# Gate and up operands of ten blocks made by GpSimd during attention and kept in DRAM, in a transformer block of attention and a gated MLP

## The chip, the cores and the metric

The kernel runs on one core of a Trainium2 chip. The metric is the device time of one execution in microseconds (us). The kernel before takes 2934.76 us, the median of three runs (2932.86 to 2934.86). The engines are called PE (matmul; PEld is its weight load), DVE (vector), ACT (scalar), POOL (GpSimd) and SP (which issues most DMAs here).

## The reference, cut to what matters

One sequence of 2048 rows with 576 features goes through a transformer block whose two normalizations are modulated by a condition `c`.

```python
mod = (silu(c) @ w_mod).reshape(1, 6, 1, -1)           # sa, ca, ga, sb, cb, gb
h = layernorm(x) * (1 + ca) + sa
x = x + ga * attention(h, wqkv, wo)                    # 32 heads of 18 features, softmax
h = layernorm(x) * (1 + cb) + sb
x = x + gb * ((sigmoid(h @ w_gate) * (h @ w_up)) @ w_down)   # 4608 hidden features
return x
```

All is float32. The kernel gets near that precision on PE's float32r format by splitting operands into a high part and a low part (the rest after rounding) and adding three products.

## The kernel before, in words

**Projections** (up to about 235 us of the span). Rows are normalized and modulated, and q, k and v are projected. q and k are kept in DRAM as high and low parts.

**Attention** is written as 32 units of 16 steps. A unit is a pair of heads and one half of the query rows; a step `kt` is one tile of 128 keys. Each step has four score products (L877), four exps on ACT (L881), the value products of earlier steps (L501) and four score products for the maxima (L411) of a later unit, each reduced by DVE (L415). PE's order is written out by hand here (`STEPS`), while the other engines' queues are filled by a scheduler from the program's order and its dependences. At the end of a unit ACT copies the accumulated values into `oT` (L515), PE transposes them, ACT copies them back into `oT` (L540) and POOL multiplies them by the reciprocals into `Oa`, or `big` in the second half (L544). `oT` has a single buffer. So L515 of a unit waits for L544 of the unit before.

Beside this, side work is handed out in turns: generators (`first_rows`, `down_parts`, `last_rows_project`) that are advanced at certain steps. `down_parts` runs from step 64 to step 240: for each of the 18 blocks of 256 hidden features POOL loads a piece of `w_down`, multiplies it by the gate `gb`, splits it and stores it in DRAM (`wds`), L779 to L801. Its loads are `paced`: they wait for the exp of the step in which they are issued. From step 240 on, the first half's rows are projected, normalized and made into operands of the MLP, with much work for POOL; the units from there on also hold the matmuls of the output projection.

**Modulation.** In units 1 and 3 the second and third part of `w_mod` are loaded, into the tiles `big` and `w0`, by `load_mod`, and used eight steps later by `modulate`.

**The MLP** runs over two halves of 1024 rows, 18 blocks of 256 hidden features each and seven products per block in the order 1, 6, 2, 7, 5, 4, 3 (`ORDER`): a Strassen-like scheme in which seven products of quarter blocks take the place of eight. Each product multiplies a weight operand (gate and up together) with a prepared row operand `X`. A weight operand is made in `weights_operand`, three products ahead (`LOOK`). In the first half `load_block` loads the raw weights; POOL makes the sums S1 to S3 (L959), ACT rounds (L970), DVE subtracts (L971, and L972 for the last 64 rows), and the result is stored in DRAM (`ws`, L973). In the second half it is loaded from `ws`. For block 0 the raw weights are loaded late in attention, and the first three operands are made behind attention's end. After two of the seven products of a block the down products of the block before are run (L1015) and added to the rows in `Oa` by DVE (L1019).

Also in the first half, `last_rows` works on the second half's rows in turns, at every odd n of the 126 products from n = 5 on: output projection, normalization, and the operands of the second half. It uses all engines, and loads pieces back from DRAM (`hs`) that it has stored.

Of the kernel before, what the change touches and what calls it, by code (L numbers as in the profile page):

```python
# [43 lines left out]
NB = F // 256  # L44
LAG = 2
# [6 lines left out]
def tile_block(ctx, tc, x_in, wqkv, wo, w_gate, w_up, w_down, c_in, w_mod, out):  # L52
# [33 lines left out]
    def load_mod(a, b, i):  # L86

        cols = slice(2 * D * i, 2 * D * (i + 1))
        for t in range(0, 4, 2):
            rows = slice(t * P, (t + 2) * P)  # L90
            nc.sync.dma_start(a[:, t : t + 2, :], w_mod[rows, cols].rearrange("(t p) c -> p t c", p=P))
        nc.sync.dma_start(b[0:64, :], w_mod[DM:D, cols])
        return [a[:, t, :] for t in range(4)] + [b]
# [218 lines left out]
    with tc.tile_pool(name="ln", bufs=2) as ln:  # L312
# [23 lines left out]
        with tc.tile_pool(name="wmp", bufs=1) as wmp:  # L336
            zs = normalized(0)
            wm = wmp.tile([P, 5, 2 * D], F32, name="wm")
            wm = load_mod(wm[:, 0:4, :], wm[:, 4, :], 0)
# [468 lines left out]
    def load_block(pool, b, k, tied=None):  # L808
# [4 lines left out]
        raw = pool.tile([P, 2, 3, 256], F32, name=f"raw{k}", bufs=1 + k)  # L813
        queue = nc.gpsimd if tied else nc.sync
# [10 lines left out]
        return raw  # L825
# [18 lines left out]
    downs = down_parts()  # L844
    for u in range(UNITS):
# [6 lines left out]
        for kt in range(NT):  # L852
# [31 lines left out]
            if u in (1, 3):  # L884
                if kt == 2:
                    a = big.tile([P, 8, 640], F32, name="big")
                    a = a.rearrange("p a b -> p (a b)")[:, 0 : 8 * D].rearrange("p (t c) -> p t c", t=4)
                    b = slots.tile([P, 2560], F32, name="w0")[:, 0 : 2 * D]
                    mods = load_mod(a, b, 1 + u // 2)
                    row = slots.tile([P, 2560], F32, name="w1")[:, 0:384]  # L890
# [4 lines left out]
            if 4 * NT <= step < FROM0 and step % 2 == 0:  # L895
                next(downs, None)
            if step == FROM0:
                for _ in downs:
                    pass
# [5 lines left out]
            if u == 30 and kt == 7:  # L905
                first = [load_block(raws, 0, k, paced) for k in range(2)]
# [4 lines left out]
            if u == UNITS - 1 and kt == 9:  # L911
# [5 lines left out]
                for i in range(2):  # L917
                    X[5 + i] = both[:, i]
                    load_x(5 + i)
    while pending:  # L920
        values()
# [20 lines left out]
    def weights_operand(st, k):  # L942
# [3 lines left out]
        kept = ws[st["b"], ORDER.index(k)]  # L946
        flat = w.rearrange("p v a c -> p (v a c)").bitcast(F32)
        if st["half"] == 1:
            nc.sync.dma_start(flat, kept.bitcast(F32))
# [11 lines left out]
        if k == 6:  # L961
            put("S1", A21, A22, ALU.add)
            put("S2", st["S1"], A11, ALU.subtract)
            put("S3", A11, A21, ALU.subtract)
# [7 lines left out]
        nc.vector.tensor_sub(w[64:P, :, 2, :], src[64:P, :, 2, :], w[64:P, :, 2, :].bitcast(F32))  # L972
# [258 lines left out]
```

## Time and profile before

| what | value |
|---|---|
| median of three runs | 2934.76 us |
| the profiled execution | 2936.12 us |
| its span, first to last instruction | 2934.3 us |
| busy: PE, DVE, ACT, POOL | 98%, 79%, 51%, 21% of the span |
| mean granted TensorE clock | 0.994 |
| first copies `oT` (L515) at steps 17, 65, 241 | 278.00, 408.05, 857.88 us |
| last copy `oT` | 1599.21 us |
| first product of the MLP | 1602.88 us |
| copy of the second half's first product | 2287.20 us |

In the rows of the profile a line names the place in the kernel, then engine, operation, `out<-in` with the tiles' names, shapes and the count; behind the bar stand the total busy time in us and the mean of one in ns, then the idle time ahead of these instructions and what ended it. In an answer by time the first column is the start in us and the second the duration; square brackets hold idle time ahead and its releaser. In an answer by stretches the columns are the stretch, its length, then the busy time and number of instructions of PE, PEld, DVE, ACT and POOL, the granted clock, the DMA engines' share and GB/s. A row on waits gives us in total, times and the longest. A row on DMA issues ends with the median us from issue to landing.

### The profile page before, as it was taken

Reading aid. Unit: us, or ns where it says so; the run is one execution under the profiler, and the core shown is the slowest. Engines: PE = TensorE matmul, PEld = TensorE weight load, DVE = VectorE, ACT = ScalarE, POOL = GpSimd, SP = SyncE. Lnnn points to the kernel's source line nnn. Section 1 sums busy time; section 2 is a strip of 40 time slices with the busy share of each in tenths; the row PEclk is TensorE's granted clock in tenths of the full one; section 3 lists DMA queues with packets and bytes.
Section 4 is the critical chain, followed back from the end, with each engine's and each line's share of the span. In section 5 each row is a group of like instructions: output and inputs, shape, how many; then the busy total and the mean of one; then the engine's idle time right before and its main releaser. Section 6 shows DMA issues by size and latency. Waiting matters only on the chain.

```text
span 2934.3 us, 46129 instructions
## 1 busy us (share of the span) xinstructions
PE 2867.2 (98%) x17141; PEld 1884.6 (64%) x17141; DVE 2305.1 (79%) x4021; ACT 1497.6 (51%) x2779; POOL 614.7 (21%) x793
## 2 busy tenths in 40 slices
PE   7999999999999999999999999998999999999999
PEld 6974333333334443443443788887888888888888
DVE  7278999999999999999992778888777555555555
ACT  3217778888887678878778333333332111111111
POOL 2001024444213110661102222233221100000000
PEclk9999999999999999999999999999999999999999
DMA  5333113333212110221125866686556854444443
GB/s 170 119 138 115 63 58 134 126 116 112 83 50 70 31 50 19 95 92 60 48 78 185 280 217 231 232 278 242 204 201 225 303 177 168 166 168 169 158 158 137
DMA packets 136089, 420.25 MB, mean 143 GB/s; under 512 B 18805, under 2 KB 56441, under 8 KB 123577
## 3 DMA queue, kind: packets, MB, share of 16 engines
q1 hardware_dynamic: 120472, 338.35, 33.7%
q0 software_dynamic: 15392, 78.95, 7.6%
q8 instruction: 135, 2.21, 0.3%
q14 instruction: 90, 0.73, 0.1%
HBM read 261.13 MB, written 155.59 MB: 142 GB/s over the span
## 4 chain that ended last, share of the span: by engine, by line
PE 85%; DVE 5%; ACT 4%; issue 3%; DMA 2%; SPq 1%; POOL 0%; ACTq 0%; DVEq 0%; POOLq 0%
PE o L501 17%; PE d L1015 14%; PE s L877 13%; PE x L979 13%; PE s L411 9%; PE bg L979 4%; PE bu L979 4%; PE s L267 4%; ACT p L881 3%; PE s L301 2%; PE s L638 2%; DVE w L971 1%; PE s L525 1%; DMA B<-hs 1%; DVE u L1163 0%
## 5 line engine op out<-in xcount | busy, mean ns | idle before, releaser
L415 DVE TENSOR_REDUCE mx<-s 128x1 f32<-128x512 f32 x2048 | 1266.9, 681 | 43.9 <-PE s L411 35.3
L881 ACT ACTIVATE p<-s 128x512 f32<-128x512 f32 x2048 | 1066.9, 607 | 268.7 <-PE s L411 145.4
L411 PE MATMUL s<-k,q 54*128 54x512 f32 x1920 | 658.0, 441 | 2.6 <-ACT p L881 1.0
L877 PE MATMUL s<-q,k 56*128 56x512 f32 x1920 | 581.5, 433 | 6.3 <-ACT p L881 0.4
L877 PEld LDWEIGHTS s<-q,k 56*128 56x128 f32 x1920 | 277.6, 185 | 469.5 <-DVE mx L415 292.6
L501 PE MATMUL o<-p,vaug 128*32 128x512 f32 x4096 | 554.4, 606 | 0.0
L1015 PE MATMUL d<-wd,hh 128*128 128x288 f32 x2304 | 470.9, 298 | 20.9 <-DVE Oa L1019 20.3
L1015 PEld LDWEIGHTS d<-wd,hh 128*128 128x128 f32 x2304 | 375.7, 189 | 35.8 <-DVE Oa L1019 27.2
L411 PEld LDWEIGHTS s<-k,q 54*128 54x128 f32 x1920 | 312.1, 185 | 80.5 <-ACT p L881 37.4
L1019 DVE TENSOR_TENSOR Oa<-Oa,d 128x288 f32<-128x288 f32 x576 | 255.9, 452 | 128.2 <-PE d L1015 123.1
L1015 PE MATMUL d<-wd,hl 128*128 128x288 f32 x1152 | 342.0, 297 | 0.0
L979 PE MATMUL x<-k,w 128*128 128x512 f32 x1008 | 245.5, 394 | 4.7 <-ACT w L970 2.4
L1015 PEld LDWEIGHTS d<-wd,hl 128*128 128x128 f32 x1152 | 218.1, 189 | 0.0
L979 PEld LDWEIGHTS x<-k,w 128*128 128x128 f32 x1008 | 188.8, 190 | 43.2 <-DVE u L1190 3.5
L991 ACT ACTIVATE u<-u 128x512 f32<-128x512 f32 x72 | 45.5, 631 | 318.7 <-DVE u L1179 312.7
L501 PEld LDWEIGHTS o<-p,vaug 128*32 128x32 f32 x4096 | 83.6, 108 | 163.7 <-issue 147.7
L988 ACT ACTIVATE sg<-x 128x512 f32<-128x512 f32 x36 | 21.5, 598 | 309.4 <-PE x L979 309.4
L1021 POOL DMA_DIRECT2D out_dram<-Oa x16 | 8.7, 542 | 606.5 <-DVE Oa L1019 606.5
L979 PE MATMUL x<-big,w 128*128 128x512 f32 x504 | 120.6, 390 | 1.0 <-issue 1.0
L979 PE MATMUL x<-w,w 128*128 128x512 f32 x504 | 121.0, 390 | 0.0
L267 PE MATMUL s<-hT,wq_h 128*128 128x512 f32 x324 | 106.1, 399 | 1.9 <-DVE hT L204 1.2
L979 PEld LDWEIGHTS x<-big,w 128*128 128x128 f32 x504 | 94.3, 188 | 21.0 <-issue 1.4
(221 smaller groups left out, 3345.2 us busy)
## 6 DMA issues: line engine op xcount, KB each, us to landing
ws<-w SPq DMA_DIRECT2D x126, 640.0 KB
w<-ws SPq DMA_DIRECT2D x126, 640.0 KB
wd<-wds SPq DMA_DIRECT2D x36, 1152.0 KB
wds<-w POOLq DMA_DIRECT2D x18, 1152.0 KB, 4.5
k<-qk SPq DMA_DIRECT2D x60, 288.0 KB
qk<-pl SPq DMA_DIRECT2D x32, 512.0 KB
w<-in_B_w_down_dram POOLq DMA_DIRECT2D x18, 576.0 KB, 4.9
q<-qk SPq DMA_DIRECT2D x64, 144.0 KB
```

The lines of the kernel that those rows point to most:

```text
L267: nc.tensor.matmul(acc, w, hT[:, t, cols], start=n == 0, stop=n == len(ts_) - 1)
L301: nc.tensor.matmul(acc[:, 0:HALF], hT[:, k, rows], w, start=n == 0, stop=n == len(ts_) - 1,)
L411: nc.tensor.matmul(sp, qs[rows, qt * P : (qt + 1) * P], ks[rows, kc * 512 : (kc + 1) * 512], start=True, stop=True,)
L415: nc.vector.tensor_reduce(mx[:, h * n + qt, kc : kc + 1], sp, axis=AX.X, op=ALU.max)
L501: nc.tensor.matmul(acc[32 * j : 32 * j + 32, :], vaug[:, kt, (2 * p + h) * VW : (2 * p + h) * VW + 32], probs[2 * c + h], start=kt == 0, s ...
L638: nc.tensor.matmul(acc[:, :HALF], a, w, start=i == 0, stop=i == len(ts_) - 1)
L877: nc.tensor.matmul(sT, ks[rows, kcols], qs[rows, c * 512 : (c + 1) * 512], start=True, stop=True)
L881: state["exp"] = nc.scalar.activation(pr, sT, AF.Exp, scale=SCALE)
L979: nc.tensor.matmul(acc[v], w[:, v, a, :], X[s][:, b, :], start=first and n == 0, stop=n == 6, skip_group_check=not first,)
L991: nc.scalar.activation(t[:, 0:512], t[:, 0:512], AF.Sigmoid)
L1015: nc.tensor.matmul(acc[:, :HALF], a[:, f, rows], w[:, f, cols], start=n == 0, stop=n == 5)
L1019: nc.vector.tensor_add(Oa[:, t, cols], Oa[:, t, cols], acc[:, :HALF])
```

## The change

1. A new generator `operands` makes the seven gate and up operands of blocks 0 to 9 (`AHEAD = 10`) on POOL alone, during attention. Per block it issues eight raw loads from POOL's queue (paced), then in seven turns the sums, the rounding, the two subtractions, and a store to `ws`. All of it lives in one tile `big` with one buffer: raw weights, sum, and one operand `w` that the next turn overwrites. Turns are given at every third step up to step 63 and at three steps of eight from step 64 to 239, 88 turns in all for 80 that hold work.
2. In the MLP's first half, blocks 0 to 9 load their operands from `ws` (`load_operand`), as the second half does. The first three operands of block 0 are loaded in the last unit of attention into the space of the raw weights.
3. Blocks 10 to 17 are made as before, but for the 64-row subtraction, which goes from DVE to POOL, and S3, which is made one operand later.
4. Since `big` is taken, modulation's weights go to the tiles `w0` and `w1` and a temporary tile.
5. `last_rows` gets a turn at two n of three, and two turns without work behind the loads from `hs`.
6. Block 0's down weights are loaded ahead of the MLP's loop.

The core of the diff:

```diff
+AHEAD = 10
...
+    def operands():
+        for b in range(AHEAD):
+            room = big.tile([P, 8, 640], F32, name="big").rearrange("p a b -> p (a b)")
+            raw = [room[:, i * 1536 : (i + 1) * 1536].rearrange("p (v t c) -> p v t c", v=2, t=3) for i in range(2)]
+            S_ = room[:, 3072:3840].rearrange("p (v t c) -> p v t c", v=2, t=3)
+            flat = room[:, 3840:5120]
+            w = flat.rearrange("p (v a c) -> p v a c", v=2, a=5)
+            for k in range(2):
+                fill_block(raw[k], b, k, nc.gpsimd, paced)
+            yield
+            A11, A12 = raw[0][:, :, :, 0:P], raw[1][:, :, :, 0:P]
+            A21, A22 = raw[0][:, :, :, P:256], raw[1][:, :, :, P:256]
+            for k, src, op, a, c in (
+                (5, S_, ALU.add, A21, A22), (6, S_, ALU.subtract, S_, A11),
+                (3, S_, ALU.subtract, A12, S_), (7, S_, ALU.subtract, A11, A21),
+                (1, A11, None, None, None), (2, A12, None, None, None), (4, A22, None, None, None),
+            ):
+                if op is not None:
+                    for v in range(2):
+                        nc.gpsimd.tensor_tensor(S_[:, v], a[:, v], c[:, v], op=op)
+                for v in range(2):
+                    nc.gpsimd.tensor_copy(w[:, v, 0:3, :].bitcast(F32R), src[:, v])
+                nc.gpsimd.tensor_sub(w[:, :, 3:5, :].bitcast(F32R), src[:, :, 0:2, :], w[:, :, 0:2, :])
+                nc.gpsimd.tensor_sub(
+                    w[64:P, :, 2, :].bitcast(F32R), src[64:P, :, 2, :], w[64:P, :, 2, :]
+                )
+                nc.gpsimd.dma_start(ws[b, ORDER.index(k)].bitcast(F32), flat)
+                yield
...
+            if step < 4 * NT and step % 3 == 0 or 4 * NT <= step < FROM0 and (step % 4 == 1 or step % 8 == 3):
+                next(ops, None)
...
-            if u == 30 and kt == 7:
-                first = [load_block(raws, 0, k, paced) for k in range(2)]
...
+                begun = {"b": 0, "half": 0}
+                for i, k in enumerate(ORDER[:LOOK]):
+                    w = raws.tile([P, 1536], F32R, name=f"raw{min(i, 1)}", bufs=1 + min(i, 1))[:, 0:1280]
+                    begun["w", k] = w.rearrange("p (v a c) -> p v a c", v=2, a=5)
+                    load_operand(begun["w", k], 0, k)
...
-        if st["half"] == 1:
-            nc.sync.dma_start(flat, kept.bitcast(F32))
+        if st["half"] == 1 or st["b"] < AHEAD:
+            load_operand(w, st["b"], k)
             return
...
-        nc.vector.tensor_sub(w[64:P, :, 2, :], src[64:P, :, 2, :], w[64:P, :, 2, :].bitcast(F32))
+        nc.gpsimd.tensor_sub(w[64:P, :, 2, :], src[64:P, :, 2, :], w[64:P, :, 2, :].bitcast(F32))
...
+                yield
+                yield
                 yield from operand_parts(1, i, blocks, parts, nc.scalar.copy, nc.vector, nc.sync)
...
-        if n >= 5 and n % 2:
+        if n >= 5 and n % 3:
             next(rows2, None)
```

What the order of the instructions shows, at three places. First POOL in attention before, between the multiplications of one unit (L544) and the next; `w_5235` is the tile in which a block of down weights is worked on:

```order
L544 TENSOR_TENSOR Oa<-oT,rec 128x8x18 x2
L779 DMA w_5235<-in_B_w_down_dram 128x2x576
L794 TENSOR_TENSOR w_5235<-w_5235,gb_b 128x288 x2
L795 CAST w_5235<-w_5235 128x288 x2
L796 TENSOR_TENSOR w_5235<-w_5235 128x288 x2
```

The same engine now, at a later unit; `big` holds the operand's parts, and lines have moved by one:

```order
L848 TENSOR_TENSOR big<-big 128x2x256
L849 TENSOR_TENSOR big<-big 64x2x128
L797 TENSOR_TENSOR w_7284<-w_7284 128x288
L852 DMA ws<-big 128x1280
L845 TENSOR_TENSOR big<-big 128x384 x2
L795 TENSOR_TENSOR w_7284<-w_7284,gb_b 128x288
L796 CAST w_7284<-w_7284 128x288
L797 TENSOR_TENSOR w_7284<-w_7284 128x288
L802 DMA wds<-w_7284 128x2304
L847 CAST big<-big 128x384 x2
```

The operands' instructions stand in one queue with those of the down weights, and a unit's multiplications behind both.

Second, ACT at the beginning of a unit now, with the semaphores that each instruction waits for (L915 is the exp, L881 before):

```order
L915 ACTIVATE p_7031<-s_7029 128x512 [waits PE_49]
L516 COPY oT<-o 128x512 [waits PE_49,Pool_49]
L915 ACTIVATE p_7042<-s_7040 128x512 [waits PE_49,Activation_49]
L915 ACTIVATE p_7052<-s_7050 128x512 [waits PE_49,Activation_49]
L915 ACTIVATE p_7059<-s_7057 128x512 [waits PE_49]
```

Before, the same copy stands at the same place with the same waits; the exps behind it stand in its queue.

Third, SP at the beginning of the MLP before, where it issues the stores of fresh operands and the loads of the next raw weights:

```order
L973 DMA ws<-w 128x1280 [waits DVE_49,DMAHW4_49,PE_49,Activation_49]
L973 DMA ws<-w 128x1280 [waits DVE_49,Activation_49]
L816 DMA raw_20722<-in_B_w_gate_dram 128x2x256 [waits DMASW6_49,DMASW1_49,DMASW7_49,DMASW0_49,Pool_49]
L818 DMA raw_20722<-in_B_w_gate_dram 128x1x256
L816 DMA raw_20722<-in_B_w_up_dram 128x2x256
```

And now:

```order
L969 DMA oend<-last 1024x1x36 [waits DMAHW3_49,DVE_49]
L856 DMA w<-ws 128x1280 x3
L1115 DMA od<-oend 128x4x192 [waits DMAHW0_49,DMAHW3_49,PE_49,Activation_49]
L1116 DMA od<-oend 128x4x64
L1137 DMA xt<-x1p 128x576 [waits DMAHW1_49]
L1137 DMA xt<-x1p 128x576 [waits DMAHW2_49]
```

The stores are gone, and the operands come as loads that wait for no DVE and no ACT.

65 lines of the change are left out of this document (37 added, 28 removed).

## The prediction

> **What bounds the kernel now.** I read the page first, then stages of equal length, then the waits of the matmul engine.
>
> ```profile
> span 2934.3 us, 46129 instructions
> PE 2867.2 (98%) x17141; PEld 1884.6 (64%) x17141; DVE 2305.1 (79%) x4021; ACT 1497.6 (51%) x2779; POOL 614.7 (21%) x793
> ```
>
> ```profile
> 450.00:492.00 42.00, 41.54 (x268) 16.80 (x272) 41.23 (x71) 35.19 (x71) 19.37 (x31) 1.00 0.35 124
> 786.00:828.00 42.00, 41.62 (x271) 16.90 (x268) 41.22 (x70) 34.84 (x70) 0.82 (x2) 1.00 0.11 33
> ```
>
> ```profile
> 1900.00:2000.00 100.00, 91.10 (x484) 79.28 (x483) 86.61 (x137) 39.51 (x62) 38.61 (x30) 0.98 0.77 275
> 2250.00:2930.00 680.00, 677.32 (x3782) 603.69 (x3780) 384.48 (x676) 119.75 (x197) 16.68 (x31) 1.00 0.52 184
> ```
>
> The columns behind each stretch are its length and the busy time of PE, weight load, DVE, ACT and POOL. PE is full nearly everywhere, but for two reasons. In attention DVE is full as well (41.2 of 42 us) and sets the step; POOL may be half busy (19.4) or idle (0.8) without a change in the 70 or 71 DVE instructions. In the first half of the MLP PE loses 8.9 us of 100, in the second 2.7 of 680. The page's 21% for POOL hides that its free time in attention is limited in every unit of 16 steps. The waits of PE in the stretch 1590:2260 are short and mostly on DVE:
>
> ```profile
> PE d L1015 <- DVE Oa L1019: 20.3, 24, 4.1
> PE x L979 <- ACT w L970: 2.4, 1, 2.4
> ```
>
> **What the MLP gains.** The copies of the first product mark each block (the first of two copies is shown), and one row of the chain gives a down product:
>
> ```profile
> 1605.78 0.58 ACT L1157 COPY p<-x 128x512 f32<-128x512 f32 x1 [2.98 <-PE x L979]
> 1635.08 0.58 ACT L1157 COPY p<-x 128x512 f32<-128x512 f32 x1
> 1794.80 0.59 ACT L1157 COPY p<-x 128x512 f32<-128x512 f32 x1
> 1908.10 0.58 ACT L1157 COPY p<-x 128x512 f32<-128x512 f32 x1
> 2069.44 0.59 ACT L1157 COPY p<-x 128x512 f32<-128x512 f32 x1
> 2251.78 0.59 ACT L1157 COPY p<-x 128x512 f32<-128x512 f32 x1
> 2287.20 0.58 ACT L1157 COPY p<-x 128x512 f32<-128x512 f32 x1
> 2881.71 0.58 ACT L1157 COPY p<-x 128x512 f32<-128x512 f32 x1
> 2291.65 6.36 PE d L1015 x48
> ```
>
> A block takes 594.51/17 = 34.97 us in the second half, where operands are only loaded, and 182.34/5 = 36.47 in blocks 12 to 16 of the first, which make them. So making costs 1.50 us a block, and blocks 1 to 9 save 13.5. Block 0 has no down product: it should take 34.97 - 2 x 6.36 = 22.25 and takes 29.30; with the wait of 2.4 above 9.4 us lie there, of which I take 8, since its three first operands now lie ready. Blocks 1 to 11 take 434.36, which is 33.2 above 11 x 36.47. That is the work on the last rows: its best stretch (blocks 5 to 7, 37.77 each) shows 1.30 of real work a block, 14.3 in all, so 18.9 are stalls. Two idle turns behind the loads and turns at two n of three instead of one of two should take about half, 9. Sum: 13.5 + 8 + 9 = 30, and with all or none of the stalls and block 0's first wait alone 16 to 42.
>
> Edits that I cost at nothing: the 64-row subtraction of blocks 10 to 17 goes from DVE to POOL, behind three products of lookahead; the third sum is made one operand later, when it is first used; block 0's down weights are loaded earlier, and no PE wait on them shows. Modulation's weights in other space are loaded at the same steps as before. If such a cover fails, block 10 waits some us once.
>
> **What attention pays.** Steps 0 to 240 get 80 turns on POOL. I price one with rows of the same shapes:
>
> ```profile
> 1595.92 1.96 POOL L959 TENSOR_TENSOR S<-raw,raw 128x384 f32<-128x384 f32 x2 [16.69 <-PE s L877]
> L612 POOL CAST t<-t 128x384 fp32r<-128x384 f32 x4 | 2.0, 506 | 6.2 <-DVE t L611 6.2
> L613 POOL TENSOR_TENSOR t<-t,t 128x512 fp32r<-128x512 f32 x8 | 10.2, 1279 | 0.7
> L626 POOL TENSOR_TENSOR t<-t,t 64x128 fp32r<-64x128 f32 x8 | 3.6, 456 | 0.6
> L816 POOL DMA_DIRECT2D raw<-in_B_w_up_dram x2: 731/736/742, 1547.6 to 1550.5; - x2
> L794 POOL TENSOR_TENSOR w<-w,gb_b 128x288 f32<-128x288 f32 x72 | 56.2, 799 | 79.2 <-DMA w<-in_B_w_down_dram 79.2
> L795 POOL CAST w<-w 128x288 fp32r<-128x288 f32 x72 | 28.4, 422 | 0.0
> L796 POOL TENSOR_TENSOR w<-w 128x288 fp32r<-128x288 f32 x72 | 56.0, 797 | 0.0
> L779 POOL DMA_DIRECT2D w<-in_B_w_down_dram x18 | 13.5, 752 | 139.6 <-ACT p L881 139.6
> L801 POOL DMA_DIRECT2D wds<-w x18 | 10.6, 590 | 5.4 <-POOL w L796 5.4
> ```
>
> One block of operands: 8 sums x 0.98 = 7.8; 14 casts x 0.506 = 7.1; 7 subtractions of 512 x 1.279 = 9.0; 7 of 64x256, between 0.456 (128 columns) and 0.799 (288), nearer the second, x 0.70 = 4.9; 7 stores x (0.59 + 5.4/18 ahead of each) = 6.2; 8 loads x 0.73 = 5.8. Together 40.8 us. A block of down weights costs POOL 170.1/18 = 9.45 (the five rows and the 5.4). Against this stands the unit of 16 steps:
>
> ```profile
> 408.05 0.59 ACT L515 COPY oT<-o 128x512 f32<-128x512 f32 x1
> 857.88 0.59 ACT L515 COPY oT<-o 128x512 f32<-128x512 f32 x1
> 458.93 0.82 POOL L544 TENSOR_TENSOR Oa<-oT,rec 128x144 f32<-128x144 f32 x2
> 445.19 0.71 POOL L779 DMA_DIRECT2D w<-in_B_w_down_dram  x1 [3.43 <-ACT p L881]
> ```
>
> The copies at steps 65 and 241 are 11 units apart: 40.89 us each. From step 64 on, 64 steps hold 3 blocks of operands, 8 of down weights and 4 pairs of Oa multiplications: 3 x 40.8 + 8 x 9.45 + 4 x 0.82 = 201.3 us of POOL in 4 x 40.89 = 163.6. That is 9.4 too much a unit before any wait. Before, POOL had time to sit idle until an exp released the next load (3.43 in the last row).
>
> The waits come on top, as there is one buffer:
>
> ```profile
> w<-in_B_w_down_dram POOLq DMA_DIRECT2D x18, 576.0 KB, 4.9
> wds<-w POOLq DMA_DIRECT2D x18, 1152.0 KB, 4.5
> xs<-t POOLq DMA_DIRECT2D x9, 512.0 KB, 3.3
> DMA to landing us min/median/max: 5.9/7.5/8.3
> ```
>
> The last row is for the four-plus-four raw loads that POOL issues before the MLP. A store of 640 KB lies between 3.3 and 4.5; I take 3.5, near the 512 KB row. By the new order, the first sums follow the eight loads nearly at once (5 us of wait a block), one store a block has nothing behind it and two have little (4), and one down load has no cover (4): 13 us a block, 9.75 a unit. POOL is then short by 19.2 us a unit.
>
> Who waits: ACT's copy oT stands before 64 exps a unit and waits for the Oa multiplications of the unit before, which stand behind all this in POOL's queue; behind ACT wait the value matmuls, the score banks and so PE and DVE. Before step 64 a block is due every 24 steps (61 us) and takes 40.8 + 17 of wait, so POOL keeps up. With three blocks (174 us) behind step 0 at 235 us, the memsets below in between, and the first down block, it ends unit 3's multiplications at about 445, 4 us before the copy at step 81 (408.05 + 40.89 = 448.9). The units 4 to 12 are then paced by POOL: 9 x 19.2 - 4 = 168 us longer. After the last turn (step 217) the old pace returns.
>
> ```profile
> 240.66 13.63 POOL L367 MEMSET k<- 32x2560 f32 x6 [156.04 <-DMA qk<-pl]
> ```
>
> Bounds: with every landing hidden only 9 x 9.4 = 85 remain, less the 32 that a unit's copy can lend at most (40.9 less some 9 from copy to multiplication, as 448.9 and 458.93 show): 53. With landings of 8.3 and 4.5, 0.8 and six times 1.0 more in each of 7.25 blocks: 49 more, 217.
>
> Two rules of the Trainium skill bear on this, and nothing above needs them. "DMA: Bandwidth & Descriptors", section "Anatomy of one DMA — SWDGE (gpsimd) path", gives about 2.0 us plus bytes over 436 GB/s for a DMA of this queue: an estimate of 3.5 for the store, as taken, but 2.6 for a 256 KB load where the row has 7.5; with its figure 5 us a block go, and 168 becomes about 132. "GPSIMD Engine Reference", section "Engine selection", speaks against the change: element-wise work with two inputs belongs on VectorE, GpSimd being about twice as slow. By the row below the same subtraction took DVE 0.840 against POOL's 1.279, so 1.5 times; with a factor of 2 a block would cost 2.8 more for these seven.
>
> ```profile
> L971 DVE TENSOR_TENSOR w<-S,w 128x512 fp32r<-128x512 f32 x72 | 60.5, 840 | 14.1 <-ACT w L970 13.7
> ```
>
> **Sum.** The profiled execution's span is 2934.3; with 2936.1 us it stands 1.4 above the median of the runs. 2934.8 + 168 - 30 = 3073.
>
> **Rivals.** (1) POOL keeps up, and only the MLP's gain is left: 2934.8 - 30 = 2905. This decides if a block costs POOL at most (163.6 - 78.9)/3 = 28.2 us with waits, against 53.8 worked out. For it: POOL is 21% busy over the span, and DVE doesn't mind it. Against it: every duration above is from a row. (2) The landings hide behind the interleaved down work, and attention is only 53 longer: 2958. For it: the order does put down work behind most stores. (3) The doubled traffic makes landings long: +217, so 3122. For it: POOL's loads now share the engines with the next heads' loads; against it: the DMA share is only 0.35 in these stretches. (4) Gain and loss cancel, which no rows suggest.
>
> **How the numbers follow.** The forecast (3000 to 3105) gets 0.68, rival 2 0.12, rival 3 0.10, rival 1 0.08, rival 4 0.02. The range goes from below rival 2 to above rival 3, 2955 to 3125. A difference within 0.2% (6 us) can't be told from no change here. Slower: 0.68 + 0.12 + 0.10 = 0.90; faster 0.08; same 0.02.
>
> **What would show it.** Right: in the changed profile the copies oT are about 60 us apart from step 81 to 225 and 41 after; ACT's copy waits for POOL's Oa multiplications; POOL is over 70% busy there; DVE falls to two thirds; block 1 of the MLP begins some 22 us after block 0, blocks 2 to 9 take 35 to 37. Wrong: copies still 41 us apart there, or a longer attention with POOL idle, or MLP blocks no shorter than 36.5.

## The result and the profile after

| | before | after |
|---|---|---|
| median of four runs | 2933.81 us (2929.06 to 2934.86) | 3140.17 us (3132.93 to 3147.07) |
| ratio, 95% interval | | 1.0706, 1.0679 to 1.0734 |
| profiled execution, its span | 2936.12, 2934.3 us | 3138.52, 3136.6 us |
| last copy `oT` (end of attention) | 1599.21 us | 1831.25 us (+232.0) |
| from there to the end of the span | 1335.1 us | 1305.3 us (-29.7) |

The time lies above the range. The sign, and the place of both the loss and the gain, are as forecast: attention 232 us longer instead of 168, the MLP 29.7 us shorter instead of 30. That second number is right by accident, as its parts show below.

From the page of the changed kernel: the span, the engines' busy time, PE's slices and the chain that ended last, by engine.

```profile
span 3136.6 us, 46204 instructions
PE 2880.8 (92%) x17141; PEld 1891.3 (60%) x17141; DVE 2200.5 (70%) x3825; ACT 1447.0 (46%) x2709; POOL 962.3 (31%) x1271
PE   7999897675587699999999999999999999999999
PE 72%; POOL 13%; DMA 10%; ACT 2%; issue 2%; DVE 1%; SPq 0%; POOLq 0%; ACTq 0%; DVEq 0%
```

PE does the same 17141 matmuls but falls from 98% to 92% of a longer span, and its holes stand in slices 7 to 14, which is attention with operand turns. POOL and DMAs together now hold 23% of the chain. Who holds whom is in the times of ACT's copies, one a unit, with the idle time ahead of each in brackets:

```profile
465.37 0.59 ACT L516 COPY oT<-o 128x512 f32<-128x512 f32 x1 [1.48 <-POOL Oa L545]
528.93 0.59 ACT L516 COPY oT<-o 128x512 f32<-128x512 f32 x1 [20.82 <-POOL Oa L545]
599.14 0.59 ACT L516 COPY oT<-o 128x512 f32<-128x512 f32 x1 [26.41 <-POOL Oa L545]
...
1045.58 0.59 ACT L516 COPY oT<-o 128x512 f32<-128x512 f32 x1 [24.27 <-POOL Oa L545]
1088.74 0.59 ACT L516 COPY oT<-o 128x512 f32<-128x512 f32 x1
1129.55 0.59 ACT L516 COPY oT<-o 128x512 f32<-128x512 f32 x1
```

From step 81 (465.37) to step 225 (1045.58) a unit takes 580.2/9 = 64.5 us, and every copy waits for POOL's `Oa` multiplications; behind the last turn the copies are 43 and then 41 us apart again. Between 440 and 1060 us ACT's wait in front of these copies and PE's wait behind ACT are nearly equal (total, times, longest):

```profile
ACT oT L516 <- POOL Oa L545: 193.8, 10, 27.9
```
```profile
PE s L911 <- ACT p L915: 195.5, 10, 28.1
```

The same nine units as one stretch, first of the changed kernel, then of the kernel before (columns: stretch, length, busy PE, PEld, DVE, ACT, POOL, granted clock, DMA share, GB/s):

```profile
465.40:1045.60 580.20, 384.18 (x2349) 152.58 (x2349) 362.11 (x605) 307.35 (x604) 421.34 (x608) 0.82 0.45 149
```
```profile
448.90:816.90 368.00, 364.63 (x2351) 146.04 (x2351) 360.76 (x604) 306.37 (x604) 149.60 (x241) 1.00 0.32 110
```

The 604 DVE instructions need the same time, but fill 62% of the stretch instead of 98%: DVE isn't slowed by POOL's work, it waits. POOL is busy for 421 of 580 us, 73%; the other 27% is what it waits for. In that stretch, POOL's waits (total, times, longest):

```profile
POOL big L847 <- DMA ws<-big: 54.5, 19, 7.3
POOL w L795 <- DMA w<-in_B_w_down_dram: 32.7, 6, 7.4
POOL big L845 <- DMA big<-in_B_w_gate_dram: 28.1, 7, 6.3
...
POOL big L817 <- DMA wds<-w: 10.0, 5, 4.2
POOL big L815 <- ACT p L915: 6.5, 2, 3.3
```

The first row is the single operand tile: the next cast waits until the store of the operand before has landed. In the MLP, the copies of the first product of blocks 0, 1, 12 and 17 answer to those shown of before:

```profile
1836.58 0.59 ACT L1204 COPY p<-x 128x512 f32<-128x512 f32 x1 [4.75 <-PE x L1024]
1859.70 0.58 ACT L1204 COPY p<-x 128x512 f32<-128x512 f32 x1
2282.11 0.58 ACT L1204 COPY p<-x 128x512 f32<-128x512 f32 x1
2457.02 0.58 ACT L1204 COPY p<-x 128x512 f32<-128x512 f32 x1
```

With the last copy `oT` and the span's end these cut the part after attention into pieces, in us. Other kernels of the experiments stand beside it:

| kernel | end of attention | to block 0's copy | block 0 | blocks 1-11 | blocks 12-16 | rest | after attention |
|---|---|---|---|---|---|---|---|
| before | 1599.2 | 6.6 | 29.3 | 434.4 | 182.3 | 682.5 | 1335.1 |
| after | 1831.3 | 5.3 | 23.1 | 422.4 | 174.9 | 679.6 | 1305.3 |
| e4, last rows' edits alone | 1601.6 | 7.1 | 28.5 | 445.1 | 182.4 | 683.0 | 1346.0 |
| e8, 64-row subtraction alone | 1599.1 | 7.1 | 30.2 | 433.8 | 174.9 | 680.3 | 1326.3 |
| e9, third sum alone | 1596.1 | 7.7 | 27.0 | 432.8 | 182.3 | 682.3 | 1332.1 |
| e10, after with the old last rows | 1835.6 | 4.2 | 23.0 | 423.8 | 174.9 | 679.1 | 1305.0 |
| e15, one block, tied, old last rows | 1598.6 | 4.2 | 34.7 | 434.0 | 174.9 | 681.6 | 1329.5 |
| e6b, five blocks, tied | 1599.3 | 4.2 | 23.1 | 444.9 | 174.9 | 684.3 | 1331.4 |
| e12, e6b with the old last rows | 1597.4 | 4.2 | 23.6 | 432.3 | 174.9 | 684.2 | 1319.2 |

Of the 29.7 us, 7.4 come before block 1, 12.0 in blocks 1 to 11, 7.4 in blocks 12 to 16, which have no operand made ahead, and 2.9 behind them.

### The profile page after: what moved, and what is told of

Read it like the earlier page. It is cut to its first block, busy times and chain, and to the rows that moved or that the text cites. A ratio compares the mean times of both kernels' runs of the same rounds, so it can differ in the third digit from the quotient of the medians.

```text
span 3136.6 us, 46204 instructions
## 1 busy us (share of the span) xinstructions
PE 2880.8 (92%) x17141; PEld 1891.3 (60%) x17141; DVE 2200.5 (70%) x3825; ACT 1447.0 (46%) x2709; POOL 962.3 (31%) x1271
## 3 DMA queue, kind: packets, MB, share of 16 engines
q0 software_dynamic: 33536, 139.05, 13.1%
## 4 chain that ended last, share of the span: by engine, by line
PE 72%; POOL 13%; DMA 10%; ACT 2%; issue 2%; DVE 1%; SPq 0%; POOLq 0%; ACTq 0%; DVEq 0%
PE x L1024 14%; PE d L1060 14%; PE o L502 10%; PE s L911 8%; PE s L412 6%; PE bg L1024 5%; PE bu L1024 5%; DMA ws<-big 4%; PE s L268 4%; POOL big L848 2%; PE s L302 2%; POOL w L795 2%; PE s L639 2%; POOL big L847 2%; POOL w L797 2%
## 5 line engine op out<-in xcount | busy, mean ns | idle before, releaser
L915 ACT ACTIVATE p<-s 128x512 f32<-128x512 f32 x2048 | 1066.8, 605 | 292.6 <-PE s L412 178.7
L911 PE MATMUL s<-q,k 56*128 56x512 f32 x1920 | 592.0, 439 | 213.7 <-ACT p L915 209.2
L412 PE MATMUL s<-k,q 54*128 54x512 f32 x1920 | 667.8, 449 | 2.6 <-ACT p L915 1.0
L502 PE MATMUL o<-p,vaug 128*32 128x512 f32 x4096 | 568.6, 621 | 0.0
L412 PEld LDWEIGHTS s<-k,q 54*128 54x128 f32 x1920 | 318.6, 188 | 78.1 <-ACT p L915 35.5
L1024 PE MATMUL x<-k,w 128*128 128x512 f32 x994 | 238.0, 390 | 0.0
L1024 PEld LDWEIGHTS x<-k,w 128*128 128x128 f32 x994 | 184.2, 188 | 36.5
L516 ACT COPY oT<-o 128x512 f32<-128x512 f32 x32 | 18.9, 590 | 209.8 <-POOL Oa L545 207.2
L268 PE MATMUL s<-hT,wq_h 128*128 128x512 f32 x324 | 106.1, 399 | 2.1 <-DVE hT L205 1.5
```

Of the source, the lines that this page charges most:

```text
L268: nc.tensor.matmul(acc, w, hT[:, t, cols], start=n == 0, stop=n == len(ts_) - 1)
L412: nc.tensor.matmul(sp, qs[rows, qt * P : (qt + 1) * P], ks[rows, kc * 512 : (kc + 1) * 512], start=True, stop=True,)
L502: nc.tensor.matmul(acc[32 * j : 32 * j + 32, :], vaug[:, kt, (2 * p + h) * VW : (2 * p + h) * VW + 32], probs[2 * c + h], start=kt == 0, s ...
L911: nc.tensor.matmul(sT, ks[rows, kcols], qs[rows, c * 512 : (c + 1) * 512], start=True, stop=True)
L915: state["exp"] = nc.scalar.activation(pr, sT, AF.Exp, scale=SCALE)
L1024: nc.tensor.matmul(acc[v], w[:, v, a, :], X[s][:, b, :], start=first and n == 0, stop=n == 6, skip_group_check=not first,)
```

## The experiments

The theory (A in the expectations): in attention POOL is over-full, by its instructions and by landings that one tile and one queue leave uncovered, and it holds the other engines through the single `oT`. Rivals: the instructions alone, the DMA traffic alone, or the order in which the turns reach POOL's queue. Once e4 and e5 were in, a theory B was formed for the MLP. Edits are to the changed kernel where nothing else is said. A time without a ratio is that of one execution; executions of the kernel before, run beside these, took from 2928.5 to 2940.2 us.

**e1, transfers alone.**
```
+            nc.gpsimd.memset(flat, 0.0)
...
-  the sums, casts and subtractions of `operands`
```


> All loads and stores of the ten blocks stay in attention, their arithmetic is left out (one memset a block instead, so the operands of these blocks are zeros; the MLP does the same instructions). Theory A (POOL's own queue, that is its instructions plus the waits between them, paces attention through ACT's copy of oT): POOL needs some 11 us a block instead of 54 and keeps pace, the copies of oT are 40.9 us apart, attention is as long as before, and the time is that of before less the MLP's 30: 2905. Rival B (the doubled DMA traffic of attention slows it, by late q and k loads): the copies stay over 60 us apart from step 81 on, 3100 or more.

Measured: 2955.63 us; attention ends at 1649.45, 50.2 us later than before. Neither figure was met: transfers alone are not free, and they are far from the whole. With no arithmetic between them the stores and loads bunch, and a piece of `w_down` lands up to 16.2 us behind POOL's need (over the whole kernel):

```profile
POOL w L795 <- DMA w<-in_B_w_down_dram: 140.0, 16, 16.2
```

Between 440 and 690 us PE also waited 13.3 us for the next heads' rows (`q` from `mrows`, 5 times, 4.5 at most), a wait that the kernel before doesn't have there, so a part of the 50 comes from transfers that hold up each other.

**e2, arithmetic without the raw loads.**
```
-            for k in range(2):
-                fill_block(raw[k], b, k, nc.gpsimd, paced)
...
-                nc.gpsimd.dma_start(ws[b, ORDER.index(k)].bitcast(F32), flat)
+                nc.gpsimd.dma_start(..., zero.unsqueeze(1).to_broadcast([P, 2, 640]))
```


> The arithmetic of the ten blocks stays, the eight raw loads a block are left out, and the seven stores a block are sent from a tile of zeros that nothing overwrites, so that no instruction of POOL waits for a landing on their account (these operands are zeros; the MLP does the same instructions). Theory A, with its two terms apart: the instructions alone are 33 us a block, 44.3 us a unit from step 64 on against 40.9, nine units owe 31 us and about as much can be lent, so attention is 0 to 15 us longer and the time 2905 to 2920; what is left of the 232 us are waits for landings. If the instructions were the greater part, the copies would be 50 us apart or more and the time over 3000. Rival C (GpSimd's access to SBUF and DVE's reductions hold each other up): the arithmetic is all there, so attention stays some 200 longer, 3100.

Measured: 3002.81 us, attention 96.8 us longer, so neither theory A nor rival C met the time. It speaks for the instructions by its number, but it is no clean test: the paced loads had also been what kept the turns at their steps. Without them the stalls stood close together (17.79, 35.19 and 33.23 us at the copies 512.61, 590.85 and 667.25) and were over by 710. Rival C is answered by the pages: DVE's reductions have a mean of 681 ns before and 680 in the changed kernel. So it was made again:

**e2b, the same, tied to the steps.**
```
+            for k in range(2):
+                paced(nc.gpsimd.memset(raw[k][:, :, :, 0:2], 0.0))
```


> Left out: the loads of the ten blocks' weights; the arithmetic works on zeros, and the stores send a tile of zeros, so no wait for a landing is left in the operands. The room is allocated once. Each block's first instruction (two small memsets) is tied to the exponential of its step as the loads were, so the instructions stand where the changed kernel has them. Theory A (instructions and waits in about equal shares: 47 us of instructions a unit against 40.9 in units 4 to 12, and 15 us of waits): GpSimd works 47 to 50 us a unit, attention ends 55 to 85 us later than before, 2955 to 2990 us. Rival (instructions alone set it, the waits would be covered): 3100 or more. Rival (POOL keeps up once nothing is waited for): 2905 to 2915.

Measured: 2968.74 us, attention 64.0 us longer, inside theory A's times. The nine units from step 81 as one stretch of e2b, POOL's wait for `w_down` in them, and the row of all its stores, whose last two times are the first and the last start:

```profile
464.30:880.90 416.60, 375.18 (x2351) 149.56 (x2351) 361.08 (x604) 307.00 (x604) 336.19 (x493) 0.94 0.29 101
```
```profile
POOL w L795 <- DMA w<-in_B_w_down_dram: 58.2, 12, 7.5
```
```profile
L855 POOL DMA_DIRECT2D ws<-zero x70: 646/686/1834, 261.3 to 421.5; - x70
```

A unit takes 46.3 us instead of 40.9. This isn't the instructions alone either. The 70 stores, which wait for no operand, were all sent before 422 us, so none stands in the nine units; 15.3 of the 64 us were lost ahead of step 81 and 48.6 in the units. There POOL is busy for 37.4 us a unit, where theory A expected 47 to 50, and the waits for `w_down` remain: only together do 336.2 and 58.2 exceed the 368 us that nine units took before. In the changed kernel POOL's instructions, with the issues of loads and stores, fill 421.3 us, 53 more than 368 before any wait. The step from 46.3 to 64.5, 18.2 us a unit, is what the operands' loads and stores add there, their issues and the waits for them together. So 168 of the 232 us appear only when the arithmetic stands beside its own transfers: e1's 50 and e2b's 64 together are 114.

**e3, two operand tiles.**
```
+            first = flat
...
+                flat = bgp.tile([P, 1280], F32, name="we") if at % 2 else first
```


> The whole work, with a second tile for the operand, used in turn, so that a store has a turn's time more before its tile is written again. Theory A: the waits for stores (106 us in the changed kernel's trace) nearly vanish, and with them 80 to 105 us of attention: 3035 to 3060. If POOL's instructions or the loads were the bound instead, little is gained: 3120 to 3140.

Measured: 3083.04 us, attention +179.4, so 53 of the 232 go: a gain between the two figures. The waits for stores fell from 54.5 to 6.1 us in the nine units (455.97 to 992.53 here) and those for raw gate weights stayed (28.3 instead of 28.1), but POOL then met the next landing in line: `w_down` 61.5 instead of 32.7.

**e7, two tiles `oT`.**
```
-            oT = epool.tile([P, 512], F32, name="oT")
+            second = half == 0 and p % 2
+            oT = (bgp if second else epool).tile([P, 512], F32, name="oT")
...
+        rec = epool.tile([P, 4, 4], F32, name="rec", bufs=2)
```


> The whole work, with oT and the reciprocals in two buffers for the first sixteen units, so that ACT may be one unit further ahead of POOL. Theory A (the lag reaches ACT through oT): the first wait of ACT comes a unit later and 30 to 41 us of attention are saved at step 240, of which some come back where the next work on POOL starts late: 3100 to 3125. If something else than oT held attention back, nothing changes: 3140.

Measured: 3098.12 us, at theory A's lower end; attention +192.7, so 39.3 go, about one unit, and the first wait (25.51) comes at the copy at 598.45. It is `oT` through which POOL holds the rest; a second tile moves that point once and adds no capacity.

**e16, stores by SyncE.**
```
-                nc.gpsimd.dma_start(ws[b, ORDER.index(k)].bitcast(F32), flat)
+                nc.sync.dma_start(ws[b, ORDER.index(k)].bitcast(F32), flat)
```


> The changed kernel with the operands' stores issued by SyncE instead of GpSimd, nothing else. GpSimd then has 7 issues of 0.56 us a block less, 4 us. Theory A (a store's landing is what one tile has to wait for, whichever queue sends it): the waits for the stores stay within a third of 106 us, and only the issues go, 7.25 blocks by 4 us: 3095 to 3130 us. Rival (the stores are late because they share GpSimd's queue with the loads): the waits for the stores fall by half or more, 3020 to 3085 us. Third (SyncE's queue holds the next heads' loads back behind the stores): PE waits for heads' loads, over 3140 us.

Measured: 3112.04 us, attention +205.4. POOL's waits for stores ahead of its casts fell over the kernel from 106.1 to 80.6 us, the longest from 7.9 to 4.0; another 13.1 us now stand ahead of raw loads. PE's and SyncE's waits between 440 and 1060 show the price:

```profile
PE s L911 <- DMA q<-mrows: 116.5, 9, 26.8
PE s L911 <- DMA k<-qk: 21.9, 2, 11.8
```
```profile
SPq L852 <- POOL big L849: 450.8, 50, 21.7
```

SyncE stands in order behind POOL's subtraction, and the heads' loads behind that. The figure is theory A's, but what the third case describes holds too, if not its time: the wait moved from `oT` to `q`, and POOL's lateness still sets the pace.

**e4, the last rows' edits alone, in the kernel before.**
```
-        if n >= 5 and n % 2:
+        if n >= 5 and n % 3:
...
+                yield
+                yield
                 yield from operand_parts(1, i, blocks, ...)
```


> The kernel before with the two edits to the last rows alone (their step is taken in two turns of three, and two empty turns stand between the loads and their use). Theory A: this is the 9 us of the MLP's gain that were put on the last rows' stalls: 2920 to 2928 us. Rival (the gain after attention comes from the ready operands alone): 2932 to 2936.

Measured: 2944.01 us, ratio 1.0032 (1.0021 to 1.0043): slower, against both expectations. Blocks 1 to 11 take 10.7 us more. PE's waits for DVE's additions are not fewer between 1590 and 2260, 23.9 us in 26 (20.3 in 24 before):

```profile
PE d L1015 <- DVE Oa L1019: 23.9, 26, 4.0
PE x L979 <- DVE u L1192: 3.6, 2, 2.4
PE d L663 <- DVE z L648: 2.6, 1, 2.6
```

**e5, one block ahead.** `AHEAD = 1`, turns at `step % 16 == 1` from step 64.

> The changed kernel with AHEAD = 1, its eight turns at steps 65 to 177, one in sixteen. Theory A: block 0's fill goes and the last rows' edits stay, 17 us of the 30, attention unchanged: 2912 to 2922 us. Rival (the ready operands of blocks 1 to 9 make most of the gain): 2926 to 2934.

Measured: 2946.01 us, ratio 1.0042 (1.0028 to 1.0056), against both expectations again: blocks 1 to 11 take 446.2 us, 11.9 more than before, while 12 to 16 take 174.9. Theory B was formed here: the last rows' edits lose time, and another edit gives 1.5 us to each block that still makes its operands.

**e8 and e9, two edits that had been costed at nothing, each alone in the kernel before.**
```
-        nc.vector.tensor_sub(w[64:P, :, 2, :], src[64:P, :, 2, :], ...)
+        nc.gpsimd.tensor_sub(w[64:P, :, 2, :], src[64:P, :, 2, :], ...)
```
```
             put("S2", st["S1"], A11, ALU.subtract)
-            put("S3", A11, A21, ALU.subtract)
+        elif k == 7:
+            put("S3", A11, A21, ALU.subtract)
```


> The kernel before with one edit: the 64-row subtraction of each operand on GpSimd instead of VectorE. The prediction put this edit at nothing. Theory B (found in the blocks of the runs so far: blocks 12 to 16 of the first half take 36.5 us in the kernel before and with the last rows' edits alone, and 35.0 wherever the changed operand code makes them): the edit takes 1.5 us off each block that makes operands, so blocks 12 to 17 take 35.0 and the part after attention is 9 to 25 us shorter: 2910 to 2926 us. Rival (making operands costs 1.5 us a block as the prediction had it, and another edit gives the 35.0): within 3 us of before.

> The kernel before with one edit: the third sum is made at operand 7 instead of operand 6. Theory B: nothing, blocks 12 to 17 stay at 36.5 us and the time within 3 us of before. Rival: this edit is the one that brings blocks 12 to 17 to 35.0, 2910 to 2926 us.

Measured: e8 2927.13 us, ratio 0.9981 (0.9971 to 0.9990); e9 2931.88 us, 0.9993 (0.9984 to 1.0003). The total of e8 lies just above theory B's range, and its part after attention is 8.8 us shorter where 9 to 25 were expected. The block times tell more than the totals, e8's copies of blocks 12 and 17:

```profile
2070.18 0.58 ACT L1157 COPY p<-x 128x512 f32<-128x512 f32 x1
2245.11 0.58 ACT L1157 COPY p<-x 128x512 f32<-128x512 f32 x1
```

174.93/5 = 34.99 us a block, with all operands still made there: the pace of the second half, where nothing is made. Making operands had cost these blocks nothing but the place of this one subtraction. In the kernel before, between 2080 and 2240, it is these rows on DVE, beside the one wait of PE:

```profile
L972 DVE TENSOR_TENSOR w<-S,w 64x256 fp32r<-64x256 f32 x17 | 7.2, 422 | 0.3
L972 DVE TENSOR_TENSOR w<-raw,w 64x256 fp32r<-64x256 f32 x13 | 5.5, 423 | 0.4
```
```profile
PE d L1015 <- DVE Oa L1019: 3.3, 8, 0.6
```

In e8 it is 2.3 to 2.5 times as long, on POOL, and PE has no wait there at all (160.00 of 160 us busy, against 156.66):

```profile
L972 POOL TENSOR_TENSOR w<-S,w 64x256 fp32r<-64x256 f32 x18 | 18.9, 1050 | 78.9 <-ACT w L970 78.6
L972 POOL TENSOR_TENSOR w<-raw,w 64x256 fp32r<-64x256 f32 x13 | 12.6, 967 | 1.0
```

**e10, the old last rows in the changed kernel** (e4's edit undone).

> The changed kernel with the last rows' turns and yields of the kernel before. The prediction put a gain of 9 us on these edits. Theory A (prediction): the part after attention is 9 us longer than in the changed kernel, 1314 us, and the time 3149. Theory B (the edits cost time, as they did alone, 11 us after attention): 1293 to 1300 us after attention, 3125 to 3135.

Measured: 3142.23 us; 1305.0 us after attention against 1305.3. Neither theory: with ten blocks ready the edits are worth nothing that shows, either way. They cost only where operands are still made beside most of the last rows: 10.7 us in blocks 1 to 11 with no block ready (e4), 12.2 with one (e5 against e15 below) and 12.6 with five (e6b against e12). That DVE's share in making them is the reason was not tried.

**e6, five blocks, thinly.** `AHEAD = 5`, turns at `step % 4 == 0` before step 64 and at `step % 7 == 1` after it.

> The changed kernel with AHEAD = 5, one turn in four before step 64 and one in seven after it. GpSimd then has 16.6 us of its other work a unit and 2.3 turns by 5 to 7 us, 28 to 33 of 40.9 us. Theory A (the end of attention moves only because GpSimd is full): attention ends at the time of before within 5 us, the MLP gains 21 to 26: 2905 to 2918 us. Rival (each store's landing holds the copies up wherever it falls): attention grows by 20 us or more, 2930 or more.

Measured: 2971.43 us, ratio 1.0114 (1.0096 to 1.0133), attention +36.5, the rival's figure. The copies were 45.05 and 55.51 us apart here, and POOL's rows in between show why; from the timeline, the stores and the multiplications, the last of them the one for which the copy at 674.20 waited:

```profile
602.40 0.56 POOL L852 DMA_DIRECT2D ws<-big  x1 [0.30 <-POOL big L849]
617.23 0.56 POOL L852 DMA_DIRECT2D ws<-big  x1 [0.30 <-POOL big L849]
617.86 0.80 POOL L545 TENSOR_TENSOR Oa<-oT,rec 128x144 f32<-128x144 f32 x2
628.82 0.59 POOL L852 DMA_DIRECT2D ws<-big  x1 [0.30 <-POOL big L849]
636.25 0.56 POOL L852 DMA_DIRECT2D ws<-big  x1 [0.30 <-POOL big L849]
649.95 0.56 POOL L852 DMA_DIRECT2D ws<-big  x1 [0.30 <-POOL big L849]
656.64 0.57 POOL L852 DMA_DIRECT2D ws<-big  x1 [0.30 <-POOL big L849]
...
673.34 0.82 POOL L545 TENSOR_TENSOR Oa<-oT,rec 128x144 f32<-128x144 f32 x2
```

Six operands in 55 us (the expectation of e6b counts seven), where the loop hands out 2.3 a unit: only the loads were paced, and nothing kept the arithmetic of a turn at its step.

**e6b, the same with every turn tied to its step.**
```
+                did = []
...
+                        did.append(nc.gpsimd.tensor_tensor(S_[:, v], a[:, v], c[:, v], op=op))
...
+                    did.append(nc.gpsimd.tensor_copy(w[:, v, 0:3, :].bitcast(F32R), src[:, v]))
+                paced(did[0])
```


> The five blocks thinly spread, and the first instruction of each operand turn tied to the exponential of its step. In the run without the tie GpSimd had seven operands within 57 us (600 to 657) where the loop gives two a unit, and the copies were 42 to 55 us apart there. Theory A (the bunching of the untied work holds the copies up, not the landings by themselves): attention ends within 8 us of before, 2932 to 2945 us, since the part after attention was as long as before. Rival (GpSimd cannot carry 2.3 turns a unit with their landings): attention stays 20 us or more longer.

Measured: 2933.35 us, ratio 1.0003 (0.9991 to 1.0015). Attention ends 0.1 us later than before: five blocks then cost nothing there. The landings are still waited for (35.4 us for stores from 446 to 816) and lie in POOL's free time.

**e14, the changed kernel with its turns tied.** The edit of e6b alone.

> The changed kernel itself, with the first instruction of each operand turn tied to the exponential of its step. Theory A (capacity: 47 us of instructions and 15 of waits a unit against 40.9): attention still 150 to 240 us longer than before, 3060 to 3140 us. Rival (the bunched order is the greater part): attention 60 to 120 us longer, 2965 to 3025 us.

Measured: 3118.32 us, attention +215.9. Its nine units from step 81:

```profile
455.70:1030.20 574.50, 383.35 (x2349) 152.59 (x2349) 361.53 (x603) 307.31 (x604) 421.56 (x608) 0.82 0.45 148
```

63.8 us a unit. With ten blocks the order is worth some 16 us of 232; the rest is capacity, instructions and waits together.

**e13, e12 and e15: seven, five and one block, tied, with the old last rows.** e13 has turns at `step % 3 == 0` and `step % 5 == 1`; e12 is e6b and e15 is e5 with tied turns, both with e4's edit undone.

> The same with seven blocks: one turn in three before step 64, one in five after it (GpSimd 33 us of 40.9 a unit, before waits). Theory A (capacity decides, and it is not yet full): attention within 15 us of before, the time 2905 to 2930 us. Rival (it is full as soon as the landings are counted, about 38 to 41 us a unit): attention 20 to 50 us longer, 2930 to 2960 us.

> Five blocks, thinly spread and tied to their steps, with the last rows' turns and yields of the kernel before. Attention as before (1599 us at its end). Theory B (block 0's fill 6 us, the 64-row subtraction 9 to 15, the last rows' edits out): 1312 to 1320 us after attention, 2911 to 2921 us. Rival (the last rows' edits pay once operands are ready, as the changed kernel's sum would have it): 1331 or more after attention, 2930 us or more.

> One block, tied, with the last rows as before. Theory B (ready operands of later blocks are worth little): within 6 us of the run with five blocks, 2915 to 2925 us. Rival (each ready block gives 1.5 us or more): 8 us or more above the run with five.

Measured: seven blocks 2994.39 us, ratio 1.0215 (1.0196 to 1.0233); five blocks 2918.60 us, 0.9958 (0.9943 to 0.9973); one block 2931.05 us, 0.9991 (0.9982 to 1.0001). The nine units of seven blocks, then of five:

```profile
464.60:891.40 426.80, 384.88 (x2344) 152.22 (x2346) 359.71 (x600) 307.13 (x603) 300.78 (x444) 0.93 0.47 153
```
```profile
446.10:815.30 369.20, 364.98 (x2351) 146.21 (x2353) 361.06 (x604) 306.71 (x605) 251.21 (x376) 1.00 0.47 156
```

With seven blocks POOL is busy 33.4 us a unit and each unit takes 47.4, so 14 us are landings and gaps; attention is 75.7 us longer, 15.7 of them ahead of step 81, beyond what either theory allowed. With five, 27.9 us busy and 41.0 a unit: free. The edge lies between them. Five blocks beat one by 12 us, where theory B had at most 6, but not by 1.5 us a block either: after attention the gain is 10.3 us, and block 0 alone gives 11.1 of gain (23.6 against 34.7), where PE waits 8.2 us for DVE with one block ready and 1.1 us for a load with five: block 0 ends early only if block 1 is ready behind it. The pieces behind it give back 0.8. The five-block version is faster than both kernels.

## Why the prediction was wrong in size

**What held.** POOL becomes the bound from step 81 to step 225 through the single `oT`, then the old pace returns; POOL is over 70% busy there (73%) and DVE is down to two thirds (62%). Prices of instructions from rows of the same shape were good. Here are those of the changed kernel for the 512 columns (1.279 taken), the two casts (0.506 each) and the 64-row subtraction (0.70):

```profile
L848 POOL TENSOR_TENSOR big<-big 128x512 fp32r<-128x512 f32 x70 | 89.2, 1275 | 4.3
L847 POOL CAST big<-big 128x384 fp32r<-128x384 f32 x140 | 67.1, 504 | 107.0 <-DMA ws<-big 106.1
L849 POOL TENSOR_TENSOR big<-big 64x256 fp32r<-64x256 f32 x70 | 50.9, 727 | 5.5
```

The lower bound of 53 us "with every landing hidden" was not put to the test: in e2b, with 64, the issues of the operands' transfers were gone from the units too, while the landings of `w_down` stayed, so it proves nothing that the two are close.

**The step that failed: "13 us a block, 9.75 a unit" of waits.** The nine units hold 54 turns, 6.75 blocks. The five rows of waits sum to 131.8 us, 19.5 a block, or 14.6 a unit. By part, in us a block: raw loads 28.1/6.75 = 4.2 (5 taken); `w_down` 32.7/6.75 = 4.8 (4 taken); stores 54.5/6.75 = 8.1 (4 taken, since two of a block's stores were to have little behind them, and the median landing was put at 3.5); the raw loads' issue behind `wds` 1.5 and pacing 1.0 (none taken). The rest of a unit, 49.9 us, is near the 50.3 that the instructions were priced at. How often POOL would wait for a store was right (19 times, 2.8 a block, for three foreseen), and so was the median landing. The step was off by the landings far above the median, as the row of all 70 stores shows:

```profile
DMA to landing us min/median/max: 3.2/3.3/10.5
```

If each of the 19 stores had landed in 3.3 us, 24 of the 54.5 us would be left, 3.6 a block. The other 30 come from later landings. Five of the 19 landed 7 to 10.5 us behind their issue, and behind four of these POOL had at once issued the next load of `w_down`, as here:

```profile
762.68 0.56 POOL L852 DMA_DIRECT2D ws<-big  x1 [0.30 <-POOL big L849]
763.24 0.72 POOL L780 DMA_DIRECT2D w<-in_B_w_down_dram  x1
764.02 1.94 POOL L845 TENSOR_TENSOR big<-big 128x384 f32<-128x384 f32 x2
773.28 0.95 POOL L847 CAST big<-big 128x384 fp32r<-128x384 f32 x2 [7.32 <-DMA ws<-big]
```

That the load holds up the store was not tried by itself.

A unit was to take 60.1 us and took 64.5: 9 x 4.4 = 40 of the 64 us that are missing. The Trainium skill's "DMA: Bandwidth & Descriptors", section "Anatomy of one DMA — SWDGE (gpsimd) path", gives an estimate of 3.5 us for such a store; the median agrees, the tail does not follow from it, and the 256 KB loads of a block, put at 2.6 each by it, landed in medians of 7.6 and 8.1. By that rule attention's growth would have come out still smaller, at 132.

**The second: "before step 64 a block ... takes 40.8 + 17 of wait, so POOL keeps up".** The copy at step 49 already waited 13.4 us for POOL's multiplications, and the copy at step 81 came at 465.37 instead of 448.94, so 16.4 us were lost by then, where 4 were to be in hand: 20 us more. Tying the turns (e14) brought that copy to 455.70, so some 10 of the 16 were the order. The remaining 3 to 4 us lie behind step 225.

**The MLP's 30: right sum, wrong terms.** "Making costs 1.50 us a block, and blocks 1 to 9 save 13.5": in blocks 12 to 16 the 1.50 was the 64-row subtraction on DVE (e8 takes it off without any operand made ahead). In blocks 1 to 11 moving that subtraction gives next to nothing (433.8 us in e8, 434.4 before), and there the ready operands are worth 10.0 us more (423.8 in e10): near 13.5, but not 1.50 in each block. "About half [of the last rows' stalls], 9": nothing that shows with ten blocks (e10), and 10.7 us lost in the kernel before (e4). Together 22.5 were expected in blocks 1 to 11, and 12.0 came, of which 2.1 are already there with five blocks ready (e12) and the rest comes with the later ones; why the later ready blocks help the last rows most was not tried. A few us are scatter: five executions with the changed kernel's MLP (the changed kernel, e3, e7, e14, e16) took from 418.3 to 422.4 us in these blocks. Against the shortfall stood "the 64-row subtraction ... from DVE to POOL" among the edits at nothing: it is worth 7.4 us in blocks 12 to 16 and 2.1 in block 17. Block 0's 8 was 7.4 with the way to it. "Blocks 2 to 9 take 35 to 37" was wrong: they take 36.7 to 40.9, since the last rows still lie in them. So the 29.7 met the 30 by luck.

The rule cited from the Trainium skill's "GPSIMD Engine Reference", section "Engine selection", that two-input work belongs on VectorE, holds here for the duration of one instruction (422 ns there, 967 to 1050 on POOL in e8) and not for the time of the kernel: in blocks 12 to 16, where DVE was late for PE and POOL had time, the slower engine was the better place.

The rivals: POOL did not keep up; the landings did not hide. Rival 3 had longer landings at 217 us, and 232 was beyond it; its reason, doubled traffic that makes every landing longer, isn't what the rows show: in the nine units the traffic rose from 110 to 149 GB/s, the medians of stores (3.3) and raw loads (7.6 and 8.1) stayed near those taken, and those of `w_down` and `wds` rose by 0.8 and 0.6 us (5.7 and 5.1); it is single late landings that cost the time. Its sum also counts 7.25 blocks in the nine units where 9.75 us a unit implies 6.75, which takes 3 us from its 217.

## What to carry to other kernels

When side work is moved to an engine with idle time, its budget is per unit of the loop that it can hold up, and with one buffer every transfer's landing counts in that budget as it falls among the other transfers, not at its median: here five blocks were free, seven cost 76 us and ten 232. Tie each piece of such work to its step, not its loads alone, or the queue fills with it ahead of what others wait for (36 us with five blocks, e6 against e6b). And a sum that comes out right is no proof of its terms: undo each edit alone, the ones costed at nothing first; here one of those (a subtraction moved off the engine that PE waits for) brought a third of the gain behind attention.

## What the runs showed of the hardware beyond that

- The granted clock fell where PE starved: 1.00 in the nine units before, 0.94 in e2b, 0.93 in e13, 0.82 in the changed kernel and in e14. The same some 2350 matmuls took 364.6, 375.2, 384.9, 384.2 and 383.4 us. Whether it cost time of its own isn't shown; where it was lowest POOL set the pace.
- Late landings of stores may go with what else is on their queue. With the loads on the same queue of POOL the longest wait for a store was 7.9 us; sent by SyncE, with the same loads and the same bytes, it was 4.0, in one execution whose order in time also differs. The Trainium skill's "DMA: Bandwidth & Descriptors", section "Queues, rings and completion order", has each DMA engine take turns between queue rows, which would fit; no run here shows the queues themselves.
- The same 64-row subtraction on POOL took 0.73 us in attention (all operands in one tile) and 0.97 to 1.05 in the MLP of e8.
